# An attention and MoE kernel: the SyncE transfer queue keeps the order of the text, and the weight conversion's transfers are stated one step later

## The chip, the cores and the metric

The kernel runs on one core of a Trainium2 chip. The metric is the device time of one execution in microseconds (us); smaller is better. The core has five engines with queues of their own: TensorE (PE, and PEld for its weight loads), VectorE (DVE), ScalarE (ACT), GpSimd (POOL) and SyncE (SP). SP computes nothing here: it issues the transfers (DMAs), one after the other, and waits at the head of its queue until what a transfer needs is there.

## The reference, cut to what matters

```python
def _attn_ref(q, k, v, f):                       # 8 batches x 8 heads x 576 x 64
    scores = scale * np.matmul(q, k.transpose(0, 1, 3, 2))
    cum = np.cumsum(np.log(np.clip(f, 0.0001, 1.0)), axis=-1)
    decay = cum[:, :, :, None] - cum[:, :, None, :]
    scores = np.where(causal, -1000000000.0, scores + decay)
    attn = softmax of scores
    return np.matmul(attn, v)

def _moe_ref(x, w_in, w_out):                    # x: 4608 x 512, w_in: 512 x 2048
    h = x @ w_in
    sp = np.maximum(h, 0.0) + np.log1p(np.exp(-np.abs(h)))
    return (h * erf(sp)) @ w_out
```

The attention's output, heads side by side, is x of the second function. The weights w_in and w_out come in as 64-bit floating point numbers. The kernel makes single-precision numbers of them and splits each into a high part that TensorE takes as it is and a low rest.

## The kernel before, in words

**Attention.** The 64 heads are taken as 32 pairs p, each in two halves, which makes 64 steps t = 2p + half in the loop at L645. A step is a row of a pipeline: step t computes the scores of t (L503), the exponentials of t-1 (L543), normalizes t-2 on POOL (L550), transposes t-3 on PE and copies the result out (L561, L572), multiplies t-4 by v (L583) and stores t-5 (L600) through the buffer xo to xt_d in DRAM. In this document a step starts with its first score matmul (L512). On DVE the order within a step is normalize's two small operations, store's copy (L606 or L609 and L610), reduce for both heads (L535), the copy of transposed blocks (L577, L575), and then the step's share of the weight conversion. The scores have two PSUM buffers, one for each head, so those of step t+1 wait for reduce of step t.

**Loads.** In an even step `load` (L468) states q, k and the decay rows c of the pair two ahead, and `load_values` (L497) states v of the pair before; v has two buffers, so its load waits until PE has finished the values of step t-5. v of pair p is read first by the values of step 2p, which run at the end of step 2p+4. `load_x` (L113) states four r transfers (the attention's output read back, L120), for the first visit in step X0 = 22 and for the second in step 63. `load_wi` (L152) for the features 0 and 1 stands in step 58.

**Weight conversion.** A feature a has four blocks u = 4a to 4a+3, two of w_out and two of w_in. Beside the attention, 46 indices of conversion work (L416) are spread over the steps by `due` (L689): index 4 comes in step 5, 5 in 6, 6 in 8, 12 in 17, 13 in 18, 20 in 29, 21 in 30. Within a feature, whose indices start at 8a: `words` (DVE, L364 to L366) of the blocks at 0, 2, 4 and 5; `joined` (DVE, L373, L382) at 1, 3, 6 and 7, which also states the load of the raw block u+2 (`load_weight`, L357, buffer wraw, two of them); `out_high` (ACT, L388) at 2 and 5 and `out_low` (POOL, L393) at 4 and 6 for w_out, each followed by a write to wo_d (L389, L394); `in_high` (ACT, L405) at 9 and 12 and `in_low` (POOL, L411) at 10, 11 and 13 for w_in, each followed by a write to wi_d (L406, L413). The buffer wtop that words writes has three places, so the fourth block's words wait until the write of the first block's low part (L394) has left its place. The buffer wa has one place: joined of a feature's third block waits for the last wi_d write of the feature before.

**MoE.** From step 64 on PE also runs units: for a visit (768 tokens) and a feature, `up` (L164) multiplies by wi, ACT and DVE apply the gate, and `down` (L225) multiplies by wo. wi and wo have two buffers each. The features 5 to 7 are converted beside the first units (L429).

**What sets the order of the work.** `manual_schedule(engines=ORDERED)` (L315) keeps the instructions of ACT, PE, DVE and POOL in the order of the text. SP is not in the set (L20): the planner of the framework places the transfers, so one may be issued far ahead of its place in the text. Each waits for its buffer and its data.

Of the kernel before, what the change touches and what calls it, by code (L numbers as in the profile page):

```python
# [11 lines left out]
F32 = mybir.dt.float32  # L12
# [4 lines left out]
ALU = mybir.AluOpType  # L17
PSUM = bass.MemoryType.PSUM
DRAM = bass.MemoryType.DRAM
ORDERED = {mybir.EngineType.Activation, mybir.EngineType.PE, mybir.EngineType.DVE, mybir.EngineType.Pool}  # L20

P = 128
B, H, S, D = 8, 8, 576, 64
NT = B * S
DM = H * D
# [32 lines left out]
NF = FF // P  # L58
NU = NF // 2
SCRATCH = 1024  # L60
X0 = 22
NU1 = 5
HALF = 3
TABLES = "natural_log_exp_and_others"
# [9 lines left out]
class Moe:  # L74
# [83 lines left out]
    def load_wo(self, u):  # L158
        if u < self.n:
            self.wo[u] = w = self.wop.tile([P, 2, 2, DM], F32R, name=f"wo{u}", tag="wo", bufs=2)  # L160
            return self.nc.sync.dma_start(out=w.rearrange("p f h e -> p (f h e)").bitcast(F32),
                                          in_=self.wo_d[self.units[u][2]])

    def up(self, u, part):  # L164
# [146 lines left out]
def attention_moe(ctx, tc, q2, k2, vp, f, w_in, w_out, out):  # L311
    nc = tc.nc
    w_in, w_out = w_in.bitcast(I32), w_out.bitcast(I32)
    ctx.enter_context(nc.allow_low_precision("float32r parts, summed to float32"))
    ctx.enter_context(tc.manual_schedule(engines=ORDERED))  # L315
    nc.scalar.preload_act_table_set(TABLES)
# [20 lines left out]
    wi_d = [dram.tile([P, 2 * 7 * 2 * P], F32, name=f"wi_d{a}") for a in range(NU)]  # L337
    wo_d = [dram.tile([P, 2 * 2 * DM], F32, name=f"wo_d{a}") for a in range(NU)]
# [5 lines left out]
    moe = Moe(tc, xt_d, out, xp, wp)  # L344
    moe.wi_d, moe.wo_d, moe.part_d = wi_d, wo_d, part_d

    raws, tops, sums, highs = {}, {}, {}, {}

    def load_weight(u):

        a, i = divmod(u, 4)
        if a == NU:
            return
        r = (2 * a + i) * P
        raw = cv.tile([P, 2 * DM], I32, name=f"wraw{u}", tag="wraw")
        raws[u] = [raw.rearrange("p (n w) -> p n w", w=2)[:, :, w] for w in range(2)]
        nc.sync.dma_start(out=raw, in_=w_in[a, i - 2] if i > 1 else w_out[r:r + P])  # L357

    def words(u):

# [25 lines left out]
    def out_high(a, i):  # L386
        highs[a, i] = hi = cv.tile([P, DM], F32R, name=f"wohi{a}_{i}", tag="wohi", bufs=1)
        nc.scalar.copy(out=hi, in_=tops[4 * a + i])  # L388
        nc.sync.dma_start(out=wo_d[a][:, 2 * i * DM:(2 * i + 1) * DM], in_=hi.bitcast(F32))  # L389

    def out_low(a, i):
        top, hi = tops.pop(4 * a + i), highs.pop((a, i))
        nc.gpsimd.tensor_tensor(out=top, in0=top, in1=hi.bitcast(F32), op=ALU.subtract)  # L393
        nc.sync.dma_start(out=wo_d[a][:, (2 * i + 1) * DM:(2 * i + 2) * DM], in_=top)  # L394

    def combine(a, *which):
        w = sums[a]
# [5 lines left out]
    def in_high(a, lo, hi):  # L403
        highs[a] = part = cv.tile([P, 4, 2 * P], F32R, name=f"whi{a}_{lo}", tag="whi", bufs=1)[:, :hi - lo]
        nc.scalar.copy(out=part, in_=sums[a][:, lo:hi])  # L405
        nc.sync.dma_start(out=wi_d[a][:, lo * 256:hi * 256], in_=part.rearrange("p i f -> p (i f)").bitcast(F32))  # L406

    def in_low(a, *which):
        for lo, hi in which:
            w = sums[a][:, lo:hi]  # L410
            nc.gpsimd.tensor_tensor(out=w, in0=w, in1=highs[a][:, lo % 4:lo % 4 + hi - lo].bitcast(F32), op=ALU.subtract)  # L411
        lo, hi = which[0][0], which[-1][1]
        nc.sync.dma_start(out=wi_d[a][:, (7 + lo) * 256:(7 + hi) * 256],  # L413
                          in_=sums[a][:, lo:hi].rearrange("p i f -> p (i f)"))

    def schedule(features):  # L416

# [24 lines left out]
        return work  # L442

    def convert(steps):
        for call, *args in steps:
            call(*args)

    moe_pools = ctx.enter_context(ExitStack())
    with ExitStack() as ph:
# [16 lines left out]
        pairs, stats, probs, vals, raw_scores, pts, banks, held = {}, {}, {}, {}, {}, {}, {}, {}  # L466

        def load(p):  # L468

            q = io.tile([P, PAD + S], F32, name=f"q{p}", tag="q")  # L470
            k = io.tile([P, S], F32, name=f"k{p}", tag="k")
            nc.sync.dma_start(out=q, in_=q2[p // NP, p % NP])
            nc.sync.dma_start(out=k, in_=k2[p // NP, p % NP])
            c = io.tile([P, 2, S], F32, name=f"c{p}", tag="c")
            if p:
                for j in range(2):
                    n = 2 * p + j
                    nc.sync.dma_start(out=c[:, j], in_=cum_d[n:n + 1].rearrange("a s -> (a s)").partition_broadcast(P))
            pairs[p] = [q, k, c]

        def lead(n):

            o = ps_o.tile([P, 512], F32, name="lead", tag="o")
            for _ in range(n):
                nc.tensor.matmul(out=o[:, :P], lhsT=ident, rhs=ident, start=True, stop=True)
# [11 lines left out]
        def load_values(p):  # L497

            v = wk.tile([P, 9, P], F32, name=f"v{p}", tag="v")
            nc.sync.dma_start(out=v, in_=vp[p // NP, p % NP].rearrange("p (c d) -> p c d", c=9))  # L500
            vals[p] = v
# [41 lines left out]
        def exps(t, j):  # L543
            st = stats[t]
            for m, i in enumerate(BLOCKS[t % 2]):
                seg = row(t, i, j)
                nc.scalar.activation(out=seg, in_=seg, func=AF.Exp, bias=st[:, 0, j, m:m + 1], scale=-1.0,  # L547
                                     accum_out=st[:, 1, j, m:m + 1])
# [71 lines left out]

        fr = wk.tile([B * H, S], F32, name="fr", tag="xo")
        nc.sync.dma_start(out=fr, in_=f.rearrange("b h s -> (b h) s"))
        load(0)
        first = wk.tile([P, 2, P], F32, name="first", tag="pr1")[:B * H]
        for j in range(2):
            nc.vector.tensor_copy(out=first[:, j], in_=ident[:B * H, j:j + 1].broadcast_to([B * H, P]))
# [1 line left out]
        cum = wk.tile([B * H, S], F32, name="cum", tag="xo")  # L628
        decay(cum, fr)
        nc.sync.dma_start(out=cum_d, in_=cum)  # L630
        load(1)
        lead(8)
        load_weight(0)
        load_weight(1)
        work = schedule(range(NU1 + 1))[:8 * NU1 + 6]
        for n in (-2, -1):
            work[n] = [step for step in work[n] if step[1] == NU1 - 1]
# [2 lines left out]
        def units(t):  # L640
            moe.up((t - NH) // 2, (t - NH) % 2)
            if t == NH + 1:
                moe.load_wi(2)

        for t in range(NH + 2):  # L645
            there = [0 <= t - n < NH for n in range(6)]
            p, half = divmod(t, 2)
            if half == 0 and t + 4 < NH:
                load(p + 2)
            if half == 0 and there[2]:  # L650
                load_values(p - 1)
            if t == X0:
                moe.load_x(0)
                moe.later = moe.x_steps(0)
            if t == NH - 6:
                moe.load_wi(0)
                moe.load_wi(1)
            if there[2]:
                normalize(t - 2)
            if there[5] and t < NH + 2:  # L660
                store(t - 5)
            if t >= NH:
                units(t)
            if there[0]:
                scores(t)
            if t == 0:
                spread(pairs[0][2], cum)
            elif t < 3:
                lead(4)
            if there[1]:  # L670
                exps(t - 1, 0)
            if there[0]:
                reduce(t, 0)
            if there[3]:
                for a in range(3):
                    transposes(t - 3, a)
                evacuate(t - 3, 0)
            if there[3] and len(BANKS[(t - 3) % 2]) == 4:
                transposes(t - 3, 3)
            if there[4]:  # L680
                values(t - 4)
            if there[1]:
                exps(t - 1, 1)
            if there[0]:
                reduce(t, 1)
            if there[3]:
                for a in range(1, len(BANKS[(t - 3) % 2])):
                    evacuate(t - 3, a)
            due = t + 1 if t < 4 else 4 + (total - 4) * (t - 3) // (NH - 2)  # L689
            at = total - len(work)  # L690
            free = 2 if at >= due else at % 8 in (1, 7)
            while work and total - len(work) < due:
                convert(work.pop(0))
            for _ in range(free if t > X0 else 0):
                convert(moe.later[:1])
                del moe.later[:1]
            if t > NH and there[4]:
                store(t - 4)
            if t == NH - 1:
                moe.load_x(1)  # L700
            if t == NH - 1:
                early.close()
                moe.ep = moe_pools.enter_context(tc.tile_pool(name="ep", bufs=2, side="right", reuse_waits="tile"))
                moe.ps_h = moe_pools.enter_context(tc.tile_pool(name="ps_h", bufs=1, space=PSUM, side="right", reuse_waits="tile"))
# [24 lines left out]
    moe.yp = ctx.enter_context(tc.tile_pool(name="yp", bufs=1, reuse_waits="tile"))  # L729
    moe.ps_y = ctx.enter_context(tc.tile_pool(name="ps_y", bufs=1, space=PSUM, reuse_waits="tile"))  # L730
    moe.load_wo(0)
    with tc.issue_after(moe.load_wo(1).ins):
        moe.load_wi(3)
    moe.want_y(0)
    work = beside_units()
    for u in range(moe.n):
        moe.middle(u, lambda u, place: convert(work.pop((u, place), ())))
        if u + 2 < moe.n:
# [2 lines left out]
            moe.combine(u, True)  # L741
            moe.up(u + 2, 1)
            moe.load_wi(u + 4)
    assert not work


# [32 lines left out]
```

## Time and profile before

| | |
|---|---|
| three runs | 1104.96, 1107.79 and 1108.95 us, median 1107.79 |
| the profiled execution | 1105.46 us, of which its span from first to last instruction is 1103.7 us |
| granted TensorE clock, mean | 0.991 |
| busy | PE 98%, DVE 76%, ACT 64%, POOL 57% of the span |
| transfers | 279.54 MB in the span, 253 GB/s |
| attention, steps 0 to 62 | 5.6 to 338.0 us |
| first units beside the last steps | 338.0 to 369.1 us |
| units alone | 369.1 to 1103.6 us |

Rows of a time line give start and length in us, the engine, the line, the operation and what it writes and reads; x counts instructions that were merged; a bracket gives the idle time of the engine before it and what ended it. `SPq` rows are issues of transfers, not the transfers. A row such as `v<-in_vp_dram SPq DMA_DIRECT2D x1, 576.0 KB, 10.8` gives the size and the us from the issue to the landing. In the views by stretch each engine has its busy us, then come the granted TensorE clock (1.00 is full), the busy share of the 16 DMA engines and the GB/s that they moved. A wait for several things is put down to the last one, and that can be a wrong name.

### The profile page before, as it was taken

To read this page: it belongs to the slowest core of one execution; us is meant where nothing else is said; L and a number is where in the kernel's file an instruction comes from. 1 tells how busy PE (TensorE), PEld (TensorE's weight loads), DVE (VectorE), ACT (ScalarE), POOL (GpSimd) and SP (SyncE) were. 2 spreads that over 40 slices of the span, in tenths; PEclk is the share of its full clock that TensorE was granted. 3 is DMA by queue.
4 is the path that set the end of the run, shared out by engine and by line. 5 is a ranking of instruction groups with operands and counts; after the bars stand their busy time and mean duration, and the time that the engine had idled before them with its cause. 6 is when DMAs were issued, how large, how long until landed. Compare 5 with 4: busy or idle time off the path is not lost.

```text
span 1103.7 us, 21942 instructions
## 1 busy us (share of the span) xinstructions
PE 1086.0 (98%) x7592; PEld 961.1 (87%) x7592; DVE 837.0 (76%) x1938; ACT 710.7 (64%) x1540; POOL 633.6 (57%) x758
## 2 busy tenths in 40 slices
PE   8999898999999999999999999999999999999998
PEld 6888787888879998899889988999889998999887
DVE  5888798899997899998767787876665766556665
ACT  4787686788777666665764666655665556545553
POOL 2667577777775887886855655744433443333322
PEclk8999999999999999999999999999999999999999
DMA  8798989888975788779677697776655655565532
GB/s 296 225 311 270 342 287 321 278 297 282 347 240 182 271 318 318 269 297 341 229 297 283 241 334 250 288 258 212 218 205 183 227 210 176 204 217 195 195 121 96
DMA packets 78462, 279.54 MB, mean 253 GB/s; under 512 B 8208, under 2 KB 21520, under 8 KB 66064
## 3 DMA queue, kind: packets, MB, share of 16 engines
q1 hardware_dynamic: 78208, 277.84, 71.5%
q8 instruction: 61, 1.00, 0.3%
q14 instruction: 49, 0.40, 0.1%
q10 hardware_dynamic: 144, 0.29, 0.1%
HBM read 231.29 MB, written 46.81 MB: 252 GB/s over the span
## 4 chain that ended last, share of the span: by engine, by line
PE 59%; DVE 0%; ACT 0%; issue 0%; DVEq 0%; ACTq 0%
PE y L233 32%; PE pha L175 8%; PE phx L175 8%; PE phy L175 8%; PE phb L175 4%; DVE wa L382 0%; ACT L206 0%; DVE u L181 0%; ACT e L206 0%; DVE ys L254 0%; DVE ys L252 0%; ACT e L204 0%; DVEq L252 0%; DVEq L214 0%; DVEq L181 0%
## 5 line engine op out<-in xcount | busy, mean ns | idle before, releaser
L222 POOL TENSOR_TENSOR gl<-e,gh 128x384 fp32r<-128x384 f32 x192 | 219.6, 1175 | 339.4 <-PE y L233 254.1
L233 PE MATMUL y<-wo,gh 128*128 128x512 f32 x1152 | 356.3, 391 | 0.2 <-DVE ys L252 0.2
L233 PEld LDWEIGHTS y<-wo,gh 128*128 128x128 f32 x1152 | 215.3, 188 | 44.2 <-DVE ys L254 1.0
L558 POOL TENSOR_SCALAR pr<-pr,st 128x576 f32<-128x576 f32 (+4 forms) x320 | 163.6, 532 | 118.2 <-DVE st L554 73.4
L233 PE MATMUL y<-wo,gl 128*128 128x512 f32 x576 | 225.3, 391 | 0.0
L254 DVE TENSOR_TENSOR ys<-y,ys 128x512 f32<-128x512 f32 x252 | 172.4, 688 | 68.3 <-PE y L233 68.2
L547 ACT ACTIVATE pr<-pr,st 128x576 f32<-128x576 f32 (+3 forms) x320 | 176.7, 557 | 6.2 <-DVE st L535 6.2
L535 DVE CUSTOM_DVE_ANT_0 pr<-s,c 128x576 f32<-128x576 f32 (+3 forms) x320 | 136.4, 486 | 27.8 <-PE s L517 19.5
L221 ACT CAST gh<-e 128x384 fp32r<-128x384 f32 x192 | 94.1, 514 | 62.2 <-DVE e L214 58.2
L233 PEld LDWEIGHTS y<-wo,gl 128*128 128x128 f32 x576 | 108.2, 188 | 22.6
L579 ACT COPY pt<-t 128x512 f32<-128x512 f32 x126 | 72.6, 577 | 77.2 <-PE t L570 74.2
L204 ACT ACTIVATE e<-u 128x384 f32<-128x384 f32 x144 | 75.0, 522 | 73.0 <-DVE u L181 71.2
L204 ACT ACTIVATE e<-pha 128x384 f32<-128x384 f32 x48 | 23.6, 492 | 152.4 <-PE pha L175 150.6
L512 PE MATMUL s<-k,q 64*128 64x320 f32 (+4 forms) x768 | 118.2, 420 | 1.8 <-DVE st L535 1.0
L175 PE MATMUL pha<-xs,wi 128*128 128x384 f32 x576 | 116.9, 338 | 0.0
L597 PE MATMUL o<-pt,v 128*64 128x128 f32 (+1 forms) x1920 | 105.1, 263 | 10.7 <-DMA v<-in_vp_dram 7.0
L175 PE MATMUL phx<-xs,wi 128*128 128x384 f32 x576 | 115.4, 335 | 0.0
L175 PE MATMUL phy<-xs,wi 128*128 128x384 f32 x576 | 115.3, 334 | 0.0
L597 PEld LDWEIGHTS o<-pt,v 128*64 128x64 f32 x1920 | 96.3, 140 | 20.4 <-issue 5.2
L512 PEld LDWEIGHTS s<-k,q 64*128 64x128 f32 x768 | 80.5, 193 | 30.3 <-issue 13.4
L175 PEld LDWEIGHTS pha<-xs,wi 128*128 128x128 f32 x576 | 102.3, 188 | 3.8
L181 DVE TENSOR_TENSOR u<-phx,u 128x384 f32<-128x384 f32 x96 | 53.3, 556 | 67.3 <-PE phx L175 66.4
(73 smaller groups left out, 1727.4 us busy)
## 6 DMA issues: line engine op xcount, KB each, us to landing
wi<-wi_d SPq DMA_DIRECT2D x48, 1792.0 KB, 7.6
wo<-wo_d SPq DMA_DIRECT2D x48, 1024.0 KB, 4.9
v<-in_vp_dram SPq DMA_DIRECT2D x32, 576.0 KB, 7.5
c<-cum_d SPq DMA_DIRECT2D x62, 288.0 KB, 6.0
r<-xt_d SPq DMA_DIRECT2D x36, 384.0 KB, 4.5
q<-in_q_dram SPq DMA_DIRECT2D x32, 320.0 KB, 5.2
k<-in_k_dram SPq DMA_DIRECT2D x32, 288.0 KB, 5.1
out_dram<-ys SPq DMA_DIRECT2D x36, 256.0 KB, 4.7
```

The costliest lines, as they stand in the source:

```text
L175: nc.tensor.matmul(out=ps, lhsT=wi[:, w, n, kd], rhs=xs[:, x, kd], start=not part and kd == 0 and i == 0, stop=kd == 1 and i == 2, skip_gr ...
L204: nc.scalar.activation(out=e_, in_=h[c], func=AF.Softplus)
L221: nc.scalar.copy(out=gh, in_=e_)
L222: nc.gpsimd.tensor_tensor(out=gl, in0=e_, in1=gh.bitcast(F32), op=ALU.subtract)
L233: nc.tensor.matmul(out=y, lhsT=x[:, cs], rhs=wo[:, i, w], start=i == 0 and n == 0, stop=i == 1 and n == 2)
L254: nc.vector.tensor_tensor(out=ys, in0=y, in1=ys, op=ALU.add)
L512: nc.tensor.matmul(out=s[j][:, at:at + k1 - k0], lhsT=q[h, PAD + START[i]:PAD + END[i]], rhs=k[h, k0:k1], start=i > 0, stop=k1 < END[i])
L535: nc.vector.tensor_tensor_reduce(out=to[:, ::-1] if j else to, in0=score, in1=decay_, scale=-0.125, scalar=BIG, op0=ALU.add, op1=ALU.min, ...
L547: nc.scalar.activation(out=seg, in_=seg, func=AF.Exp, bias=st[:, 0, j, m:m + 1], scale=-1.0, accum_out=st[:, 1, j, m:m + 1])
L558: nc.gpsimd.tensor_scalar(out=seg, in0=seg, scalar1=st[:, 2, j, m:m + 1], scalar2=1.0, op0=ALU.mult, op1=ALU.mult)
L579: nc.scalar.copy(out=pt[:, 512 * a:512 * a + 512], in_=b)
L597: nc.tensor.matmul(out=o[h, to:to + width], lhsT=v[:, ch, h], rhs=pt[:, at[j]:at[j] + width], start=n == 0, stop=n == len(parts) - 1, skip ...
```

## The change

SP joins the ordered set, so the transfers are issued in the order of the text. The transfers of the weight conversion are no longer stated where their operation stands. `transfer` puts them on a list, and `queue_transfers` states all that is on the list: at the start of each step, behind that step's v, q, k and c, and at the start of each `convert`. `load` is cut in two (`load_decays` states c), v is stated ahead of q and k, the loads of the first steps are stated in another order, X0 is 23, and wi 3 needs no `issue_after`.

```diff
-ORDERED = {mybir.EngineType.Activation, mybir.EngineType.PE, mybir.EngineType.DVE, mybir.EngineType.Pool}
+ORDERED = {mybir.EngineType.Activation, mybir.EngineType.PE, mybir.EngineType.DVE, mybir.EngineType.Pool,
+           mybir.EngineType.SP}
...
-X0 = 22
+X0 = 23
...
+    def transfer(out, in_):
+        moves.append((out, in_))
+
+    def queue_transfers():
+        for out, in_ in moves:
+            nc.sync.dma_start(out=out, in_=in_)
+        moves.clear()
...
     def load_weight(u):
-        nc.sync.dma_start(out=raw, in_=w_in[a, i - 2] if i > 1 else w_out[r:r + P])
+        transfer(raw, w_in[a, i - 2] if i > 1 else w_out[r:r + P])
...
     def out_low(a, i):
-        nc.sync.dma_start(out=wo_d[a][:, (2 * i + 1) * DM:(2 * i + 2) * DM], in_=top)
+        transfer(wo_d[a][:, (2 * i + 1) * DM:(2 * i + 2) * DM], top)
...
     def convert(steps):
+        queue_transfers()
         for call, *args in steps:
             call(*args)
...
-        load(0)
+        for p in range(2):
+            load(p)
+        load_decays(0)
+        for u in range(2):
+            load_weight(u)
+        queue_transfers()
...
         nc.sync.dma_start(out=cum_d, in_=cum)
-        load(1)
+        load_decays(1)
         lead(8)
-        load_weight(0)
-        load_weight(1)
...
+            if half == 0 and there[2]:
+                load_values(p - 1)
             if half == 0 and t + 4 < NH:
                 load(p + 2)
-            if half == 0 and there[2]:
-                load_values(p - 1)
+                load_decays(p + 2)
+            queue_transfers()
             if t == X0:
                 moe.load_x(0)
...
     moe.load_wo(0)
-    with tc.issue_after(moe.load_wo(1).ins):
-        moe.load_wi(3)
+    moe.load_wo(1)
+    moe.load_wi(3)
```

`out_high`, `in_high` and `in_low` are changed as `out_low` is. The stores of xt_d, the r loads, wi and wo are stated where they were.

More of the change, by code (lines that the diff above doesn't have):

```diff
@@ L160, in load_wo @@
             self.wo[u] = w = self.wop.tile([P, 2, 2, DM], F32R, name=f"wo{u}", tag="wo", bufs=2)
-            return self.nc.sync.dma_start(out=w.rearrange("p f h e -> p (f h e)").bitcast(F32),
+            self.nc.sync.dma_start(out=w.rearrange("p f h e -> p (f h e)").bitcast(F32),
                                           in_=self.wo_d[self.units[u][2]])
@@ L345, in attention_moe @@
     moe.wi_d, moe.wo_d, moe.part_d = wi_d, wo_d, part_d
-    raws, tops, sums, highs = {}, {}, {}, {}
+    raws, tops, sums, highs, moves = {}, {}, {}, {}, []
+    def transfer(out, in_):
[4 more added lines that the diff above has]
+        moves.clear()
     def load_weight(u):
@@ L388, in out_high @@
         nc.scalar.copy(out=hi, in_=tops[4 * a + i])
-        nc.sync.dma_start(out=wo_d[a][:, 2 * i * DM:(2 * i + 1) * DM], in_=hi.bitcast(F32))
+        transfer(wo_d[a][:, 2 * i * DM:(2 * i + 1) * DM], hi.bitcast(F32))
     def out_low(a, i):
@@ L405, in in_high @@
         nc.scalar.copy(out=part, in_=sums[a][:, lo:hi])
-        nc.sync.dma_start(out=wi_d[a][:, lo * 256:hi * 256], in_=part.rearrange("p i f -> p (i f)").bitcast(F32))
+        transfer(wi_d[a][:, lo * 256:hi * 256], part.rearrange("p i f -> p (i f)").bitcast(F32))
     def in_low(a, *which):
@@ L412, in in_low @@
         lo, hi = which[0][0], which[-1][1]
-        nc.sync.dma_start(out=wi_d[a][:, (7 + lo) * 256:(7 + hi) * 256],
-                          in_=sums[a][:, lo:hi].rearrange("p i f -> p (i f)"))
+        transfer(wi_d[a][:, (7 + lo) * 256:(7 + hi) * 256], sums[a][:, lo:hi].rearrange("p i f -> p (i f)"))
     def schedule(features):
@@ L473, in load, with load_decays @@
             nc.sync.dma_start(out=k, in_=k2[p // NP, p % NP])
+            pairs[p] = [q, k]
+        def load_decays(p):
             c = io.tile([P, 2, S], F32, name=f"c{p}", tag="c")
@@ L478, in load @@
                     nc.sync.dma_start(out=c[:, j], in_=cum_d[n:n + 1].rearrange("a s -> (a s)").partition_broadcast(P))
-            pairs[p] = [q, k, c]
+            pairs[p].append(c)
         def lead(n):
@@ L743, in attention_moe @@
             moe.load_wi(u + 4)
-    assert not work
+    assert not work and not moves
 def kernel(q, k, v, f, moe_w_in, moe_w_out):
```

## The prediction

> **What bounds the kernel now.** On the page TensorE is busy nearly all the time, so I read the busy time by stretch first, to find where it is not, and then the time line of the stretches that stood out.
>
> ```profile
> core 0: us, PE busy (x) PEld busy (x) DVE busy (x) ACT busy (x) POOL busy (x), PEclk, DMA share, GB/s
> 5.60:338.00 332.40, 321.02 (x3614) 268.94 (x3614) 289.08 (x1036) 253.37 (x771) 223.82 (x373) 0.97 0.86 291
> 369.10:1103.60 734.50, 730.72 (x3661) 660.08 (x3660) 526.08 (x843) 434.87 (x722) 391.77 (x353) 1.00 0.66 237
> 47.09:56.94 9.85, 9.85 (x124) 8.27 (x120) 8.11 (x32) 7.60 (x25) 6.89 (x12) 1.00 0.80 216
> 116.59:131.94 15.35, 11.31 (x123) 9.63 (x119) 8.33 (x34) 7.59 (x25) 6.74 (x13) 0.89 1.02 347
> 183.11:198.78 15.67, 12.72 (x124) 10.33 (x120) 10.43 (x37) 7.59 (x25) 9.36 (x15) 0.78 0.99 364
> 300.13:313.00 12.87, 10.35 (x124) 8.84 (x120) 9.94 (x34) 8.43 (x26) 8.36 (x16) 1.00 1.00 348
> ```
> The MoE stretch (369.10 on) has 3.8 us of idle TensorE in 734.5: nothing to win there. The attention stretch runs 63 steps in 332.40 us. Two undisturbed steps (47.09 to 56.94, steps 8 and 9) take 9.85 us, so 31.5 such pairs would take 310.3: at most 22 us can be won by any order of transfers. The last three rows are the worst pairs, steps 22 and 23, 34 and 35, 56 and 57. They exceed 9.85 by 5.50, 5.82 and 3.02.
>
> The time line says what they waited for (start, length, in brackets the idle time before; TensorE, then VectorE):
>
> ```profile
> 124.09 2.83 PE L597 MATMUL o<-pt,v 128*64 128x128 f32 x28 [4.04 <-DMA v<-in_vp_dram]
> ```
> ```profile
> 189.52 2.83 PE L597 MATMUL o<-pt,v 128*64 128x128 f32 x28 [2.95 <-DMA v<-in_vp_dram]
> ```
> ```profile
> 304.64 0.69 DVE L382 SCALAR_TENSOR_TENSOR wa<-wraw,wtop 128x512 int32<-128x512 int32 x1 [2.35 <-DMA wi_d<-wa]
> ```
> Twice it is v, once a write of converted weights. The transfer queue shows why v was late (start of issue; below it, KB and us from issue to landing):
>
> ```profile
> 111.12 0.32 SPq L155 DMA_DIRECT2D wi<-wi_d  x1
> ...
> 175.91 0.32 SPq L155 DMA_DIRECT2D wi<-wi_d  x1
> ...
> 178.60 0.41 SPq L500 DMA_DIRECT2D v<-in_vp_dram  x1
> 179.06 0.45 SPq L615 DMA_DIRECT2D xt_d<-xo  x1
> 179.60 0.41 SPq L357 DMA_DIRECT2D wraw<-in_w_out_dram  x1
> ```
> ```profile
> v<-in_vp_dram SPq DMA_DIRECT2D x1, 576.0 KB, 10.8
> wraw<-in_w_out_dram SPq DMA_DIRECT2D x1, 512.0 KB, 11.8
> ```
> The text of the kernel loads wi 0 and 1 in step 58, but without SP in the ordered set they were issued in steps 20 and 32, each ahead of that step's v, with the queue's head held until the writes of wi_d had landed.
>
> **The change part by part.** *v first, wi back in step 58.* Both v now go out at the start of steps 20 and 32. Step 20 starts two steps before 116.59, at some 106.7: even with the 10.8 us above its v lands by 117.6, and TensorE asks at 124.09 - 4.04 = 120.05. Step 32 starts two steps before 183.11, at some 173; v lands by 184, wanted at 186.57. Both stalls go: -5.50 and -5.82. What would be next in these steps is VectorE, 8.11 us busy of 9.85: no new limit. The r transfers of the second visit (step 63 in the text, issued before step 56) leave the queue ahead of the weight write, so I take its 2.35 us as gone too, of 3.02 (bounds 0 and 3.02). Sum of the gains: 13.7.
>
> *Conversion transfers one step later.* They are now behind v, q, k and both c in an even step. Most have time. One has not: words for the fourth block of a feature (L364) writes the one wtop buffer of three that is free only when out_low's write of it (L394) has landed, and out_low runs one conversion index, thus one or two steps, earlier. By the formula for due that is step 5 for step 6, 17 for 18, 29 for 30, 40 for 42, 52 for 54. In the first three the write comes out in an even step, the very one that needs it. Step 6 before:
>
> ```profile
> 37.24 1.57 PE L512 MATMUL s<-k,q 64*128 64x320 f32 x12
> ```
> ```profile
> 36.87 0.32 SPq L394 DMA_DIRECT2D wo_d<-wtop  x1
> ...
> 39.20 0.38 SPq L500 DMA_DIRECT2D v<-in_vp_dram  x1
> ```
> ```profile
> wo_d<-wtop SPq DMA_DIRECT2D x1, 256.0 KB, 2.9
> ```
> ```profile
> v<-in_vp_dram SPq DMA_DIRECT2D x1, 576.0 KB, 6.5
> ```
> ```profile
> 41.82 0.42 DVE L364 TENSOR_SCALAR wtop<-wraw 128x512 int32<-128x512 int32 x1
> ```
> The write was first of six (wtop, q, k, c, c, v) and landed at 39.8, two us before L364 wanted it; the sixth landed at 45.7, 8.8 after the first issue. After the change the same six go out from the step's start, 37.24, with the write last: 37.3 + 8.8 = 46.1, and VectorE stands 4.3 us. The Trainium skill, "DMA: Bandwidth & Descriptors", section "Queues, rings and completion order", says that each DMA engine consumes its ring in order, while completions need not be in order; these two landings agree with an order kept.
>
> What a stand of VectorE costs TensorE shows in step 18, which had one:
>
> ```profile
> 102.45 0.43 DVE L364 TENSOR_SCALAR wtop<-wraw 128x512 int32<-128x512 int32 x1 [1.47 <-DMA wo_d<-wtop]
> ```
> ```profile
> 96.32:101.19 4.87, 4.87 (x62) 4.11 (x58) 4.55 (x18) 4.67 (x15) 3.12 (x6) 1.00 0.69 195
> 106.17:111.61 5.44, 5.44 (x62) 4.49 (x58) 4.71 (x20) 3.93 (x14) 4.48 (x8) 1.00 0.82 321
> 162.09:166.96 4.87, 4.87 (x61) 4.10 (x58) 4.77 (x17) 4.67 (x15) 3.18 (x5) 1.00 0.72 208
> ```
> 1.47 us made step 20 0.57 longer than 4.87: 0.9 is hidden (normalize, reduce and the two score buffers are queued behind words; scores two steps on wait for reduce). In the 304.64 case nothing was hidden; I take 0.9. Step 6 costs 3.4. In steps 18 and 30 index 12 and 20 also put a whi write ahead, so seven transfers count:
>
> ```profile
> 163.19 0.32 SPq L394 DMA_DIRECT2D wo_d<-wtop  x1
> ...
> 165.99 0.42 SPq L500 DMA_DIRECT2D v<-in_vp_dram  x1
> ```
> ```profile
> v<-in_vp_dram SPq DMA_DIRECT2D x1, 576.0 KB, 8.2
> ```
> ```profile
> 167.65 0.99 DVE L364 TENSOR_SCALAR wtop<-wraw 128x512 int32<-128x512 int32 x1
> ```
> First issue to last landing: 174.2 - 163.2 = 11.0. Step 18: 96.4 + 11.0 = 107.4 against 102.45 - 1.47 = 101.0, so 6.4, less 0.9, less the 0.57 it cost before: 4.9. Step 30: 162.2 + 11.0 = 173.2 against 167.65: 5.5, less 0.9: 4.6. For odd steps (41, 53) the conversion's transfers are first in the queue: nothing.
>
> *Two wi in step 58.* They stand ahead of store's xt_d write of pair 26, whose buffer (xo, two of them) VectorE refills in step 61 (L606):
>
> ```profile
> 329.50 0.42 DVE L606 COPY xo<-o 128x256 f32<-128x256 f32 x1
> ```
> ```profile
> 315.29 0.33 SPq L357 DMA_DIRECT2D wraw<-in_w_out_dram  x1
> ```
> ```profile
> wi<-wi_d SPq DMA_DIRECT2D x1, 1792.0 KB, 7.5
> ```
> ```profile
> v<-in_vp_dram SPq DMA_DIRECT2D x1, 576.0 KB, 3.9
> ```
> The queue from 175.91 held one wi, q, k, c, c, v, xo and wraw and was done at 191.4, after 15.5 us. Step 58 has the same and a second wi: from an idle queue wi takes 7.5 and v 3.9, so 1216 KB cost 3.6 and 1792 KB 5.3. Step 58 started at 313.00, and its queue is held until joined releases wraw, 315.29: 315.3 + 15.5 + 5.3 = 336.1, a stand of 6.6, cost 5.7. If nothing holds the queue and wraw is out of it (1.2), the stand is 3.2: cost 2.3.
>
> *The clock.* After the 4.04 us stall of step 22 the clock was halved:
>
> ```profile
> 123.70:127.10 3.40, 3.01 (x30) 2.92 (x32) 0.15 (x1) 0.00 (x0) 2.49 (x5) 0.50 1.07 305
> ```
> That is the 5.50 - 4.04 = 1.46 us on top. The 2.95 us idle was followed by a clock of 0.78 over the pair, the 2.35 one by none. The four new stalls are 3.4 to 5.7 us, each cut in two by the first head's scores; I take 3 x 1.46 = 4.4, bounds 0 and 5.8. The Trainium skill, "TensorE: Matmul & The Clock Gate", section "Why this matters for your kernels", warns of gaps over about 3 us; by that rule for all four the sum would be 1.4 more, and the 2.95 us case agrees.
>
> *The rest.* At the start, cum goes out ahead of two transfers and c of pair 1 sooner; the first steps are not waiting for them in these rows: 0, bounds -1 and +1. X0 = 23 changes no x step, only the r loads, read from step 24 on: 0. In the MoE stretch the late writes stand behind stores; cover is VectorE's 208 us of idle there; 0 to +2, taken 0.
>
> Sum: -13.7 + 3.4 + 4.9 + 4.6 + 5.7 + 4.4 = +9.3. The profiled execution took 1105.46 us, 2.33 under the median of the three runs (1107.79), inside their spread. Forecast 1105.46 + 9.3 = 1114.8, say 1115.
>
> **The rivals.** *Faster: the moved write still lands in time.* The place is L364 in steps 6, 18 and 30, the price 12.9 us and three clock drops. It decides at 5.5 us after the step's start (41.82 - 37.24 = 4.6, and 0.9 hidden): a write landed by then costs nothing. For it: the DMA engines were busy only 0.80 of steps 8 and 9, so the six may be slow by their issue and not by the engines. Against it: from an idle queue v alone takes 3.9, which leaves 1.6 for five more. Then: 1105.46 - 13.7 + 5.7 + 1.5 = 1099.0.
>
> *No change: sizes at the low end.* With v, q, k, c and c done 2 us sooner the three cost about 7, the store 2.3, and the clock stays: 1105.46 - 13.7 + 7 + 2.3 = 1101 at the very least; with the middle sizes but no clock drop 1110. For it: stalls in two pieces. Against it: after 2.95 us idle the clock did fall. Centre 1106.
>
> *The order hardly differs.* If the queue kept issuing as before, 1105.5. Against it: the wi at 111.12 stood some 200 us ahead of its place in the text.
>
> **How the numbers follow.** 0.5% is 5.5 us, about what a measurement of this kernel can tell from no change. Forecast as sized, slower: 0.49, own range 1108 to 1121 (high end: each late landing 1 us later, all four clock drops). Low sizes: 0.26, and order kept: 0.04, together 0.30 for no change. Covered write: 0.21, faster. The range 1097 to 1121 reaches into the faster case and leaves out its far part (store's stall covered too, 1092) and a tenth above.
>
> **What would show it.** Right: steps 22, 34 and 56 near 4.9 us; L364 waiting 4 to 6 us on wo_d<-wtop in steps 6, 18 and 30; L606 waiting on xt_d in step 61; half clock after each. Wrong: no wait at L364, or stalls on v remaining, or idle TensorE after step 63.

## The result, and the profile after

The changed kernel took 1119.92 us (median of four runs, 1116.37 to 1121.94), the kernel before 1106.88 us beside it (1104.96 to 1108.95): a ratio of 1.0114, 95% interval 1.0077 to 1.0151. The change costs 13 us. The profiled execution of after took 1116.37 us with a span of 1114.6; the one of before had 1103.7, so the two traces differ by 10.9.

The busy time by stretch, for the changed kernel, with the stretches cut at the first scores of a step as in the prediction (columns as there: bounds and length, then busy time of each engine, granted clock, share of the DMA engines):

```profile
core 0: us, PE busy (x) PEld busy (x) DVE busy (x) ACT busy (x) POOL busy (x), PEclk, DMA share, GB/s
5.57:348.01 342.44, 320.62 (x3613) 269.30 (x3613) 290.79 (x1039) 253.75 (x771) 225.62 (x373) 0.97 0.84 280
379.10:1114.50 735.40, 730.63 (x3662) 659.88 (x3660) 524.74 (x843) 435.02 (x722) 392.03 (x353) 1.00 0.66 237
...
39.29:48.17 8.88, 5.43 (x67) 4.49 (x63) 3.88 (x17) 5.59 (x18) 2.15 (x4) 0.95 0.55 175
...
103.62:115.66 12.04, 6.41 (x67) 5.50 (x63) 4.82 (x21) 5.78 (x18) 3.97 (x8) 0.86 0.59 195
125.50:135.34 9.84, 9.84 (x123) 8.26 (x119) 8.26 (x34) 7.59 (x25) 6.80 (x13) 1.00 0.91 251
170.42:182.14 11.72, 6.54 (x66) 5.99 (x62) 5.79 (x24) 6.51 (x19) 5.61 (x10) 0.78 0.53 201
...
192.80:202.65 9.85, 9.85 (x123) 8.31 (x119) 9.68 (x34) 7.59 (x25) 7.50 (x12) 1.00 0.68 221
305.31:315.94 10.63, 10.35 (x123) 8.84 (x119) 9.98 (x34) 8.33 (x26) 8.37 (x15) 1.00 0.86 261
330.86:342.10 11.24, 6.44 (x67) 5.50 (x63) 5.16 (x19) 6.72 (x19) 4.28 (x8) 0.79 0.88 354
```

The three pairs of steps for which the prediction forecast a gain have become short: 22 and 23 (125.50) and 34 and 35 (192.80) take 9.84 and 9.85 us where they took 15.35 and 15.67, and 56 and 57 take 10.63 for 12.87. In their place four single steps are long: 7, 19, 31 and 61, with 8.88, 12.04, 11.72 and 11.24 us, where such a step takes 4.98 undisturbed. In three of the four the DMA engines are only 0.53 to 0.59 busy, but that is an average of two parts. In step 19 they were 0.95 busy until the transfer waited for had landed, and idle after it:

```profile
103.62:110.70 7.08, 3.46 (x34) 2.63 (x30) 0.00 (x0) 4.14 (x12) 1.11 (x2) 1.00 0.95 314
110.70:115.66 4.96, 2.95 (x33) 2.86 (x33) 4.82 (x21) 1.64 (x6) 2.86 (x6) 0.66 0.06 25
```

VectorE's time line shows who stood (start, length, in brackets the idle time before it and what ended it; the first of the four has no releaser that the profile could name):

```profile
44.19 0.43 DVE L374 TENSOR_SCALAR wtop<-wraw 128x512 int32<-128x512 int32 x1 [5.11 <-issue]
...
110.70 0.43 DVE L374 TENSOR_SCALAR wtop<-wraw 128x512 int32<-128x512 int32 x1 [7.29 <-DMA wo_d<-wtop]
...
176.80 0.43 DVE L374 TENSOR_SCALAR wtop<-wraw 128x512 int32<-128x512 int32 x1 [5.58 <-DMA wo_d<-wtop]
...
338.64 0.42 DVE L620 COPY xo<-o 128x256 f32<-128x256 f32 x1 [6.01 <-DMA xt_d<-xo]
```

And TensorE's time line at the same places:

```profile
46.20 0.44 PE L611 MATMUL o<-pt,v 128*64 128x128 f32 x4 [3.45 <-DVE xo L620]
...
112.71 0.70 PE L611 MATMUL o<-pt,v 128*64 128x128 f32 x4 [5.63 <-DVE xo L620]
...
179.17 0.48 PE L611 MATMUL o<-pt,v 128*64 128x128 f32 x2 [5.18 <-DVE xo L620]
...
339.12 0.70 PE L611 MATMUL o<-pt,v 128*64 128x128 f32 x4 [4.80 <-DVE xo L620]
```

Read the two together: words (L374) waits for the write of wtop; behind it on VectorE is store's copy xo<-o (L620), which empties the single buffer o; and the next values need o. So each stand of VectorE reaches TensorE in one piece, 19.06 us in all.

The whole span by stretches, between the first scores of the named steps, for both kernels and the runs below (us, one profiled execution each; the last column is the span):

| kernel | to 6 | 6-18 | 18-22 | 22-30 | 30-34 | 34-56 | 56-58 | 58-63 | after 63 | span |
|---|---|---|---|---|---|---|---|---|---|---|
| before | 37.2 | 59.1 | 20.3 | 45.5 | 21.0 | 117.0 | 12.9 | 25.0 | 765.7 | 1103.7 |
| after | 34.4 | 64.3 | 26.7 | 40.1 | 27.2 | 112.5 | 10.6 | 32.1 | 766.6 | 1114.6 |
| changed_again | 36.0 | 64.7 | 26.1 | 40.1 | 27.5 | 112.3 | 10.6 | 30.1 | 766.5 | 1114.0 |
| wtop_at_once | 38.2 | 59.1 | 20.2 | 40.0 | 20.8 | 112.7 | 10.6 | 31.3 | 766.7 | 1099.5 |
| wtop_fourth | 36.3 | 59.1 | 19.9 | 40.0 | 21.1 | 112.3 | 10.6 | 31.2 | 766.5 | 1097.0 |
| wi_58_60 | 36.1 | 64.3 | 26.4 | 40.0 | 27.5 | 112.2 | 10.6 | 25.0 | 766.9 | 1109.0 |
| both | 37.7 | 59.1 | 19.9 | 40.0 | 20.8 | 112.6 | 10.6 | 25.0 | 766.9 | 1092.5 |
| v_last | 39.4 | 61.2 | 23.8 | 40.0 | 24.7 | 112.2 | 10.6 | 30.6 | 766.7 | 1109.2 |
| v_third | 34.5 | 59.1 | 22.2 | 40.0 | 21.0 | 112.7 | 10.6 | 31.5 | 766.6 | 1098.2 |
| order_alone | 40.8 | 59.4 | 20.0 | 40.0 | 21.1 | 114.0 | 11.3 | 32.7 | 765.7 | 1105.0 |
| all_at_once | 41.2 | 59.1 | 20.0 | 40.0 | 20.8 | 112.9 | 10.9 | 30.5 | 765.7 | 1101.0 |
| filled_stalls | 40.0 | 63.7 | 24.9 | 40.0 | 25.3 | 112.6 | 10.6 | 30.8 | 766.8 | 1114.8 |
| all_early | 38.0 | 59.1 | 20.1 | 40.2 | 21.0 | 113.4 | 11.9 | 25.0 | 765.5 | 1094.2 |

The first column is to be read with care: the first six steps of one and the same code took 34.4 to 40.0 us from run to run. The granted clock goes with it. The two shortest starts, 34.4 (after) and 34.5 (v_third), had the full clock throughout; the other starts of that code have a mean of 0.84 to 0.89, and so has before:

```profile
5.61:37.24 31.63, 30.66 (x223) 23.55 (x223) 21.96 (x86) 18.66 (x60) 11.47 (x21) 0.84 0.73 261
5.57:34.42 28.85, 27.04 (x223) 20.13 (x223) 21.98 (x86) 18.66 (x60) 11.51 (x21) 1.00 0.78 287
```

The stretches 22-30 and 34-56 agree within 0.6 us in the runs that keep the delay, a stretch with a stall within 2.

### The profile page after: what moved, and what is told of

It reads as the page before. It is cut to its first block, busy times and chain, and to the rows that moved or that the text cites. A ratio compares the mean times of both kernels' runs of the same rounds, so it can differ in the third digit from the quotient of the medians.

```text
span 1114.6 us, 21911 instructions
## 1 busy us (share of the span) xinstructions
PE 1085.9 (97%) x7592; PEld 961.6 (86%) x7592; DVE 836.9 (75%) x1938; ACT 711.2 (64%) x1540; POOL 635.7 (57%) x758
## 4 chain that ended last, share of the span: by engine, by line
PE 79%; DMA 5%; DVE 3%; issue 0%; ACT 0%; SPq 0%; POOL 0%; DVEq 0%; ACTq 0%; POOLq 0%
PE y L234 34%; PE pha L176 9%; PE phx L176 9%; PE phy L176 9%; PE o L611 5%; PE s L526 4%; PE phb L176 4%; PE t L584 4%; DMA xt_d<-xo 1%; DMA wo_d<-wtop 1%; PE s L531 1%; DVE pr L549 1%; DMA v<-in_vp_dram 1%; DMA r<-xt_d 1%; DMA wi_d<-wa 1%; DVE wtop L383 1%
## 5 line engine op out<-in xcount | busy, mean ns | idle before, releaser
L611 PE MATMUL o<-pt,v 128*64 128x128 f32 (+1 forms) x1920 | 107.0, 266 | 20.3 <-DVE xo L620 19.3
L526 PEld LDWEIGHTS s<-k,q 64*128 64x128 f32 x768 | 80.6, 192 | 30.0 <-issue 13.7
```

What stands on the lines that cost most here:

```text
L526: nc.tensor.matmul(out=s[j][:, at:at + k1 - k0], lhsT=q[h, PAD + START[i]:PAD + END[i]], rhs=k[h, k0:k1], start=i > 0, stop=k1 < END[i])
L611: nc.tensor.matmul(out=o[h, to:to + width], lhsT=v[:, ch, h], rhs=pt[:, at[j]:at[j] + width], start=n == 0, stop=n == len(parts) - 1, skip ...
```

## The experiments

Each edit is against the changed kernel, order_alone against the kernel before.

**The changed kernel once more (changed_again).**

> The changed kernel itself, unchanged, beside the two runs below. My theory: the stalls stand in every run (steps 7, 19, 31 and 61 between 8.5 and 12 us), and the early start of its profile (step 6 at 34.42 us, no halved clock in the first 20 us) was one draw: step 6 at 36 to 40 us here as in the eight runs with the same start, and a median of 1117 to 1121. Rival (the first four times were taken on a slower chip, and v last gains nothing): a median of 1111 to 1114.

1118.18 us (four runs, 1115.74 to 1120.84), ratio 1.0100 [1.0062, 1.0137]. The four stalls are there again, step 6 starts at 35.95. So the runs below are to be measured against 1118 to 1120 us, and after's early start was a draw, not an effect of the change.

**wtop's write at once (wtop_at_once).**

```
     def out_low(a, i):
...
-        transfer(wo_d[a][:, (2 * i + 1) * DM:(2 * i + 2) * DM], top)
+        nc.sync.dma_start(out=wo_d[a][:, (2 * i + 1) * DM:(2 * i + 2) * DM], in_=top)
```

> The changed kernel, but out_low's write of wtop goes to the queue where it is computed, and not one step later. My theory (three late writes of wtop, in steps 6, 18 and 30, are most of the loss): L374 no longer waits for wo_d<-wtop, steps 7, 19 and 31 fall from 8.88, 12.03 and 11.73 us to 5, the half clock after them goes, the stall on xt_d in step 61 stays: 18 us less than the changed kernel, about 1100. Rival A (the order itself costs: SP now stands at the write until GpSimd has made it, and v, q, k, c behind it come late): the waits at L374 go, but waits on v, q or c of 3 to 5 us appear in steps 6 to 56, and the time stays over 1110. Rival B (the buffers are not the limit, VectorE is late for another reason): L374 goes, the time stays within 3 us of 1118.

1099.34 us (ten runs), ratio 0.9943 [0.9923, 0.9962]. The three stalls are gone (6-18, 18-22 and 30-34 in the table), the fourth stands where it stood, and no new wait on v, q or c came. Rivals A and B fall; one line moved by one step was worth 19 to 21 us. What is left, on VectorE's time line of this run:

```profile
323.44 0.42 DVE L620 COPY xo<-o 128x256 f32<-128x256 f32 x1 [5.35 <-DMA xt_d<-xo]
```

**One wi each in steps 58 and 60 (wi_58_60).**

```
-            if t == NH - 6:
-                moe.load_wi(0)
-                moe.load_wi(1)
...
                 store(t - 5)
+            if t in (NH - 6, NH - 4):
+                moe.load_wi((t - NH + 6) // 2)
```

> The changed kernel, but wi 0 is loaded in step 58 behind the store of that step, and wi 1 in step 60 behind the store. My theory (two wi ahead of the write of xt_d hold the xo buffer that step 61 needs): L620 no longer waits 6.0 us for xt_d, step 61 falls from 11.23 us to 5.0 and step 62 from 5.91 to 4.9, all else stays: 7 us less than the changed kernel, about 1112. Rival: the wi now delay the write of step 60 and the v of step 60, and a stall of 3 to 5 us moves to step 62 or 63: within 3 us of the changed kernel.

1110.85 us (ten runs), ratio 1.0043 [1.0019, 1.0067]: 7 to 9 less than the changed kernel. The stretch 58-63 takes 25.0 us, as before the change, and nothing moved to step 62 or 63.

**Both edits (both).**

> The two edits together, wtop's write at once and one wi each in steps 58 and 60. My theory: the two gains add, since the stalls lie 150 us and more apart: 25 us less than the changed kernel, about 1093, some 13 less than the kernel before, whose two stalls on v and one on wi_d stay away. Rival: what was gained comes back as stalls on v or c, or in the MoE stretch: 1100 or more.

1093.42 us (four runs), ratio 0.9882 [0.9844, 0.9921]: 12 us faster than the kernel before. The gains add within the spread of the runs, as they should for stalls so far apart. This version beats both kernels.

**A fourth buffer instead of an earlier write (wtop_fourth).**

```
-        tops[u] = top = cv.tile([P, DM], F32, name=f"wtop{u}", tag="wtop", bufs=3)
+        tops[u] = top = (cv if u >= 16 else tp).tile([P, DM], F32, name=f"wtop{u}", tag="wtop",
+                                                    bufs=3 if u >= 16 else 4)
...
+        tp = early.enter_context(tc.tile_pool(name="tp", bufs=4, side="right"))
```

> The changed kernel with every transfer in its place, but a fourth buffer for wtop while the weights of the first four features are converted. My theory (the queue's order does not cost by itself, it costs because words needs the buffer): the waits at L374 in steps 6, 18 and 30 go although the writes land as late as before, 18 us less than the changed kernel, about 1100, within 3 us of the run with wtop's write at once. Rival (the late writes hold something else next, the single buffers of wohi and whi that ScalarE refills): ScalarE and then words wait 2 to 4 us in steps 7, 19 and 31, and less than half of the gain comes.

1099.47 us (ten runs), ratio 0.9953 [0.9929, 0.9977], the same as with the write moved. The writes land as late as in the changed kernel (a median of 7.1 us after their issue, for 7.3), and it costs nothing: the loss is the wait for a buffer, not the order of the transfers as such.

**v behind q, k and c again (v_last).**

```
-            if half == 0 and there[2]:
-                load_values(p - 1)
             if half == 0 and t + 4 < NH:
                 load(p + 2)
                 load_decays(p + 2)
+            if half == 0 and there[2]:
+                load_values(p - 1)
             queue_transfers()
```

> The changed kernel with v stated behind q, k and c of its step again, as before. My theory (the two stalls on v came from the wi ahead of it, not from v's place in the step): v has two steps and 3.5 us, 13 us, and its step's transfers need 9 to 11, so no wait on v; the waits at L374 and in step 61 stay within 1 us: within 3 us of the changed kernel (1117 to 1122). Rival (v first took the stalls away): steps 22 and 34 wait 3 to 4 us on v again and the clock halves, 9 to 11 us more, about 1130.

1112.54 us (ten runs), ratio 1.0040 [1.0016, 1.0063]: 6 to 7 us less than the changed kernel, where I expected no difference. As expected, no stall on v came back: v's place in the step was not what removed them. Not expected was that the stalls got shorter. The waits of SP, the engine that issues the transfers, show why (what it waited for at which line: us in total, times, longest). First the changed kernel, then this one:

```profile
SPq L514 <- PE o L611: 108.4, 27, 8.8
```

```profile
SPq L514 <- PE o L611: 10.4, 4, 4.7
```

L514 is the issue of v. v has two buffers, and the one that it goes to is read by the values of the step just before. Stated first, v stands at the queue's head until those matmuls end, in 27 of its 32 loads, and q, k, c and the conversion's writes stand behind it, though q's and k's own buffers are free some 3 us earlier. In the kernel before this wait occurs once (6.0 us).

**A third buffer for v (v_third).**

```
-            v = wk.tile([P, 9, P], F32, name=f"v{p}", tag="v")
+            v = (v3 if p % 3 == 2 else wk).tile([P, 9, P], F32, name=f"v{p}", tag="v", bufs=1 if p % 3 == 2 else 2)
...
+        v3 = early.enter_context(tc.tile_pool(name="v3", bufs=1, side="right"))
```

> The changed kernel, v first, with every transfer in its place, but a third buffer for v. My theory after the run with v last (v stated first waits at the queue's head until the values of the step before have read the buffer it goes to, and q, k, c and the conversion's writes wait behind it): SP no longer waits for TensorE's o at v, the write of wtop goes out 1 to 3 us earlier in steps 6, 18 and 30, steps 7, 19 and 31 come to 6.4, 8.1 and 8.4 us as with v last, each within 1 us, step 61 too gets shorter by up to 1: 7 us less than the changed kernel. Rival (what counts is v's 576 KB ahead of the others, not the wait at it): no change, steps 7, 19 and 31 at 8.5 to 12.

1099.76 us (ten runs), ratio 0.9939 [0.9915, 0.9964]. SP's wait for o at v is gone, as stated, but the size is not the one expected: 18 to 20 us, not 7. No transfer was moved in the text, and two of the three stalls are gone, the third is 1.78 us of TensorE. SP's time line around step 18 (start and length of each issue), for the changed kernel, in which the step starts at 98.76, and for this one, in which it starts at 93.53:

```profile
98.87 0.33 SPq L514 DMA_DIRECT2D v<-in_vp_dram  x1
99.25 0.49 SPq L482 DMA_DIRECT2D q<-in_q_dram  x1
99.79 0.42 SPq L483 DMA_DIRECT2D k<-in_k_dram  x1
100.31 0.85 SPq L492 DMA_DIRECT2D c<-cum_d  x2
101.26 0.38 SPq L356 DMA_DIRECT2D wi_d<-whi  x1
101.74 0.74 SPq L356 DMA_DIRECT2D wo_d<-wtop  x1
```

```profile
88.00 0.38 SPq L515 DMA_DIRECT2D v<-in_vp_dram  x1
90.33 0.33 SPq L483 DMA_DIRECT2D q<-in_q_dram  x1
90.71 0.42 SPq L484 DMA_DIRECT2D k<-in_k_dram  x1
92.99 1.08 SPq L493 DMA_DIRECT2D c<-cum_d  x2
94.25 0.32 SPq L356 DMA_DIRECT2D wi_d<-whi  x1
94.66 0.38 SPq L356 DMA_DIRECT2D wo_d<-wtop  x1
```

v is under way 5.5 us before the step instead of 0.1 after it, so the DMA engines have its 576 KB behind them when the write of wtop comes. Relative to the step the write goes out only 1.9 us earlier, but words gets its buffer 3.8 us earlier (101.62 - 93.53 = 8.1 after the step's start, for 110.70 - 98.76 = 11.9):

```profile
101.62 0.43 DVE L374 TENSOR_SCALAR wtop<-wraw 128x512 int32<-128x512 int32 x1 [3.43 <-DMA wo_d<-wtop]
```

The rest is that the write lands sooner once it is issued. The median of all such writes from issue to landing, in the changed kernel and here, is

```profile
wo_d<-wtop SPq DMA_DIRECT2D x16, 256.0 KB, 7.3
```

```profile
wo_d<-wtop SPq DMA_DIRECT2D x16, 256.0 KB, 4.9
```

So three conditions had to meet: a v that can't start before the step and whose 576 KB go ahead of the write, the write one step late and behind it, and a consumer of that buffer in the same step. The third buffer for v, the write at once and the fourth buffer for wtop each take one of them away, and each gives 18 to 21 us back. Stating v last takes away most of the wait at the queue's head (10.4 us are left of 108.4) but leaves v's bytes ahead of the write, and it gives 6 to 7 us. That speaks for a part of this run's rival, that v's bytes count; no run tries them apart from the wait. Nor does the wait at v cost by itself. With the write at once SP still stands there, and that run is as fast as this one:

```profile
SPq L514 <- PE o L611: 72.0, 22, 5.7
```

**The kernel before with the order kept and nothing else (order_alone).**

```
-ORDERED = {mybir.EngineType.Activation, mybir.EngineType.PE, mybir.EngineType.DVE, mybir.EngineType.Pool}
+ORDERED = {mybir.EngineType.Activation, mybir.EngineType.PE, mybir.EngineType.DVE, mybir.EngineType.Pool,
+           mybir.EngineType.SP}
...
-    with tc.issue_after(moe.load_wo(1).ins):
-        moe.load_wi(3)
+    moe.load_wo(1)
+    moe.load_wi(3)
```

> The kernel before with nothing but the order kept: SP in the ordered set (and the three loads at the start of the MoE stretch as the changed kernel states them); v last in a step, the conversion's transfers where they are computed, both wi in step 58. My theory: the gains of 13.7 us come from wi's return to step 58 alone, the stall on xt_d in step 61 comes with it (7 us), no waits at L374: about 1099. Rival (without the step of delay SP stands at what GpSimd and ScalarE have not made yet and holds q, k, c, v behind it): new waits on q, c or v of 2 us and more, 1107 or slower.

1105.12 us (ten runs), ratio 0.9990 [0.9971, 1.0008]: no change, where I expected 1099. The two stalls on v and the one on wi_d are gone and step 61 has its stall, as forecast. A part of the rest went where I had not expected it, to the start: wraw of the first two blocks is stated behind cum and c there, and VectorE stands for it in step 1.

```profile
17.25 0.43 DVE L365 TENSOR_SCALAR wtop<-wraw 128x512 int32<-128x512 int32 x1 [6.11 <-DMA wraw<-in_w_out_dram]
```

Step 6 starts at 40.8, and steps 34 to 58 take 2.2 us more than in the changed kernel, with waits of TensorE of 1 us and less. The reordered start of the change, which the prediction priced at nothing, takes away a wait that the kept order alone brings. What that is worth one trace does not show: the starts of one code differ by 5.5 us, and 40.8 is only 0.8 above the longest of them.

**Every conversion transfer at once (all_at_once).**

```
     def transfer(out, in_):
...
-        moves.append((out, in_))
+        nc.sync.dma_start(out=out, in_=in_)
```

> The changed kernel with v first, but every transfer of the conversion goes to the queue where it is computed, not one step later. My theory (of the delayed transfers only the writes of wtop have a consumer near): the same as with wtop's write alone at once, 1099 within 3 us, step 61 still 10 to 11 us. Rival (the delay is what keeps SP from standing at unfinished products): v, q, k or c come 2 us and more later than there, steps of over 6 us in the first 56, and the time is 1104 or more.

1099.93 us (ten runs), ratio 0.9947 [0.9929, 0.9966], the same as with wtop's write alone. Of all the delayed transfers only those of wtop mattered in the attention stretch. After step 63 this run takes 765.7 us, as before the change, where the delayed versions take 766.5 to 766.9: the delay costs 1 us in the MoE stretch.

**TensorE kept busy in the stalls (filled_stalls).** The added matmuls write a bank that nothing reads.

```
+            for _ in range({7: 5, 19: 9, 31: 9, 61: 8}.get(t, 0)):
+                fill(t)
             if there[4]:
                 values(t - 4)
```

> The changed kernel with work added that nothing reads: 5, 9, 9 and 8 matmuls of 128x128 float32 ahead of the values of steps 7, 19, 31 and 61, about 0.47 us each, 2.4 to 4.2 us in each of the four stalls; the waits of VectorE stay as they are. My theory (the stall itself halves the clock, and of the loss 8 us are the slower matmuls after it): the granted clock stays at 1.0 in steps 7, 8, 19, 31, 32, 61 and 62, those steps shorten by 1.4 to 2.5 us for each stall: 8 us less than the changed kernel, about 1112. Rival (the clock falls for another reason, or the matmuls only add time): no change or slower, 1119 to 1128, the half clock stays.

1115.83 us (six runs), ratio 1.0073 [1.0046, 1.0100]: 2 to 4 us less than the changed kernel. In the stretches 6-18, 18-22, 30-34 and 58-63 it takes 144.7 us for 150.4 and 148.4 in the two runs of the changed kernel, so 3.7 to 5.7 less. The clock stayed at 1.0 at three of the four places. At the fourth, step 61, it fell, after 2.02 us of idle time: the eight added matmuls took 2.05 us there (the row counts two for each), 0.26 each for the 0.47 that I had counted, and filled half of the stall.

```profile
335.61 2.05 PE L507 MATMUL fill<-ident 128*128 128x128 f32 x16
339.68 1.84 PE L619 MATMUL o<-pt,v 128*64 128x128 f32 x32 [2.02 <-DVE xo L628]
```

The direction was right, the expected 8 us were not reached. At the other three places the matmuls left 2.73, 2.37 and 2.71 us idle in one piece, more than the 2.02 that cost the clock at the fourth, so there it was in part luck that the clock stayed (the last section says what decided).

**What did not pay, undone (all_early).** The edits of v_last, all_at_once and wi_58_60 together.

> Everything of the change that did not pay undone: conversion transfers where they are computed, v behind q, k and c, one wi each in steps 58 and 60 behind the store; the order kept and the start as in the changed kernel. My theory: no stall over 1 us from step 6 on, the MoE stretch 1.0 us shorter than with the delay (765.7 for 766.9 us after step 63): about 1092, 1 to 2 under the run with both edits (1093.4). Rival (SP stands at what GpSimd has not made yet, with q and k behind it): steps 40 to 57 longer by 2 to 3 us, 1095 or more.

1095.00 us (four runs), ratio 0.9890 [0.9851, 0.9929], not to be told from the run with two edits. The MoE stretch gains the 1 us; steps 34 to 58 lose 2.0, as its rival forecast. TensorE's waits in these steps come to 2.8 us, the longest 1.2, for 0.6 in the run with both edits; which transfer stands behind them stays open.

## Why the prediction was right

The forecast was +9.3 on the profiled execution; the traces differ by +10.9, the medians of the first comparison by +13.0. By its steps, with the differences of the table (unrounded):

| step | forecast | measured |
|---|---|---|
| v and wi, steps 22-23, 34-35 | -5.50, -5.82 | 22-30: -5.45; 34-35: -5.82 |
| weight write, step 56 | -2.35 | -2.24 |
| wtop late, 6-18 | +3.4 | +5.26 with the clock |
| wtop late, 18-22 | +4.9 | +6.47 with the clock |
| wtop late, 30-34 | +4.6 | +6.23 with the clock |
| two wi, 58-63 | +5.7 | +7.09 with the clock |
| clock | +4.4 | about 6.5 |
| start | 0 | -2.8 in this draw |
| MoE | 0 | +0.9 |

*The gains* came to about the tenth of a us, except that the other steps from 36 to 55 took 1.3 us more. The reason given with them, "v first, wi back in step 58", was half wrong: in v_last and order_alone v stands behind q, k and c and the stalls are gone all the same, so wi's return did it. X0 = 23 was not tried by itself.

*The late writes.* VectorE stood 5.11, 7.29 and 5.58 us where 4.3, 6.4 and 5.5 were forecast, and the idle time of TensorE, 3.45, 5.63 and 5.18, agrees with forecasts of 3.4, 5.5 and 4.6. The way from one to the other was not the one forecast: the prediction has the scores two steps on wait for reduce, and the rows show the values waiting for o. So the 0.9 us taken as hidden were 1.66, 1.66 and 0.40. wtop_at_once and wtop_fourth show the cause of the stand from two sides. What the prediction did not say is why the transfers go out only "from the step's start": it took that start as given. The description of the loads has v wait for the values of step t-5, but the working does not use it for a v that stands at the queue's head. v's wait for TensorE, 108.4 us in 27 places, is the reason, and the one such wait of before could have warned of it. The size came out right by luck, in that the assumption happened to be what v's wait enforces.

*The store in step 61* stood 6.01 us for 6.6. wi_58_60 shows the cause.

*The clock* is the term that was too small. The step that failed is "each cut in two by the first head's scores": TensorE's rows above show one piece each, since the queue of work goes through xo and the single buffer o. All four places had half the clock in part (granted clocks of 0.78 to 0.95 in their steps). The stretches grew by 25.0 us, and with the 0.57 that step 20 cost already by 25.6, of which 19.1 is idle time: 6.5 for the clock and for catching up, above the upper bound of 5.8. filled_stalls, with three of the four drops gone, got 3.7 to 5.7 back.

*The start* was taken as nothing within 1 us. That can't be told from one profile, since it varies by 5.5 us from run to run; the profile of after drew the shortest of all, with no halved clock, while before had 0.84. That fits traces that differ by less (10.9) than the medians (13.0). So the forecast of 9.3 is closer to 10.9 than it deserves: without the -2.8 of the draw the rest adds up to 13.7.

*The MoE stretch* lost 0.9 of the 0 to 2 forecast. VectorE waits for the write of wa, works without a pause from there to the copy ys<-y, and TensorE waits for that copy. In all_at_once, without the delay, the first wait is not there and the second is 0.2 us:

```profile
457.47 0.69 DVE L392 SCALAR_TENSOR_TENSOR wa<-wraw,wtop 128x512 int32<-128x512 int32 x1 [1.74 <-DMA wi_d<-wa]
```

```profile
463.54 0.50 PE L234 MATMUL y<-wo,gh 128*128 128x512 f32 x1 [1.20 <-DVE ys L253]
```

*The rivals.* The covered write fell: words needed its buffer 4.6 us after the step's start and got it after 9.8 to 11.9. v_third shows what it would have taken: with the earlier v the writes do land in time in steps 6 and 30, and the time is 1099.76, for the 1099.0 worked out for that rival. The low sizes and the kept order fell with the rows above.

## What to carry to other kernels

Before a transfer is put at the head of an ordered queue, ask when its own destination becomes free: the queue waits there, and everything behind it waits too, whether or not it was ready. Whether that costs anything depends on how soon something behind it is needed. A late write costs nothing until someone needs its source buffer, so look for the consumer with the fewest spare buffers, and try the extra buffer against the reordering: here one buffer more for either of two tiles was worth as much as moving the write. And a change that bundles an order, a delay and a placement can hide a gain: two small edits to it turned 1.1% slower into 1.2% faster.

## What the runs showed of the hardware

In each trace the granted clock changes on a grid of 3.41 us. In that of the changed kernel it fell to half at 47.29, 112.14, 177.00 and 337.42 us, which are 19, 19 and 47 times 3.413 us apart, and it stayed there for 3.41 or 6.83 us. In these runs it fell after a slot of the grid with some 2 us of idle time. The rows below are pairs of neighbouring slots; the idle time of a slot is its length less TensorE's busy time. Before, the 2.5 us idle at step 56 fell on two slots, 1.02 and 1.51, and the clock stayed:

```profile
301.20:304.61 3.41, 2.39 (x23) 1.82 (x19) 1.10 (x1) 2.48 (x12) 0.55 (x1) 1.00 1.00 364
304.61:308.02 3.41, 1.90 (x29) 1.70 (x30) 3.34 (x14) 2.46 (x7) 2.20 (x4) 1.00 0.97 278
```

With v last, 2.44 us fell into one slot, and the next has half the clock:

```profile
108.72:112.13 3.41, 0.97 (x17) 0.82 (x17) 2.73 (x11) 1.93 (x6) 0.99 (x2) 1.00 0.95 324
112.13:115.54 3.41, 3.41 (x30) 2.88 (x28) 2.61 (x15) 1.34 (x6) 2.87 (x7) 0.50 0.27 88
```

With the filled stalls 2.02 us in one slot were enough:

```profile
337.60:341.01 3.41, 1.39 (x29) 1.33 (x30) 1.81 (x8) 0.95 (x4) 0.74 (x1) 1.00 1.03 406
341.01:344.42 3.41, 3.41 (x24) 2.79 (x20) 3.29 (x14) 0.83 (x4) 0.26 (x1) 0.50 0.86 210
```

In the thirteen profiles, from 20 to 1000 us, every full-speed slot with 1.99 us idle or more is followed by half the clock (1.99 is before's slot from 185.15), and none with 1.79 or less is (1.79 is v_third's from 317.01). The longer gaps that filled_stalls left, 2.73, 2.37 and 2.71 us, fell on two slots each, with at most 1.61 us in one. The Trainium skill, "TensorE: Matmul & The Clock Gate", section "Why this matters for your kernels", warns of gaps over about 3 us, one window of idle; here 1.99 us in one slot halved the clock and a gap of 2.73 us across two slots did not, so by these runs the place of the gap in the grid decides between 2 and 3 us.

The wait of v at the queue's head agrees with the Trainium skill, "Perfetto Trace Analysis", section "Per-engine timelines", which puts the semaphore wait of such a transfer into the sequencer that issues it, ahead of the next instruction: SP waited 108.4 us at v, and q, k and c went out 0.4 to 0.5 us apart right behind it.
